# Halving the columns of the backward products with transposed weights

## The chip, the cores and the metric

One core of a Trainium2 chip runs the whole program in one launch. The metric is the device time of that core in microseconds, from the runs below. The core has TensorE (matrix products into PSUM), VectorE, ScalarE, GpSimd, and SyncE, whose queue issues most DMAs. In the profile they are PE, DVE, ACT, POOL and SP; PEld is TensorE's loading of weights, which overlaps its products.

## The reference, cut to what matters

The kernel computes a forward pass and all its gradients. A layer norm of x feeds two branches that are added: a recurrent attention over 64 segments of 32 rows, with 32 heads of 128 and a memory of 8 rows, and a dense layer with a squared ReLU.

```python
mem = mem0
for s in range(n_seg):                       # 64 segments
    h = concatenate([mem, xs], axis=1)       # 8 + 32 rows of 512
    q, k, v = (einsum('btd,dhe->bhte', h, W) for W in (Wq, Wk, Wv))
    p = softmax(where(mask, einsum('bhqe,bhke->bhqk', q, k) * scale, -1e9))
    o = einsum('bhte,hed->btd', einsum('bhqk,bhke->bhqe', p, v), Wo)
    mem = o[:, :M]                           # goes into the next segment
    outs.append(o[:, M:])
out = x + A(layernorm(x)) + B(layernorm(x))
grads = vjp(grad_out)                        # of x, mem0, all weights and biases
```

Backward, the gradient of a segment's memory rows is needed before the segment ahead of it can be begun, so the 64 segments are again a chain. What the change touches is the gradient of h: for each segment the sum over the three projections t and the 32 heads of d(q, k or v) times the transposed weight of that head.

## The kernel before, in words

Four stages follow each other: the dense branch with the layer norm (0 to 330 us of the profile), the forward recurrence with the weight gradients of the dense branch between its steps (to 1390), the backward recurrence (1398 to 2556), and the weight gradients of the attention with the backward layer norm (to the end).

In each of the middle stages the work is handed to a planner (`_Plan`) as operations with an engine or a choice of engines, a cost, the keys that they read and write, and a priority. The planner lists them by cost and due time, and that list is the program order of every engine. Where a choice of ScalarE or VectorE is given, it picks. The costs are written in the code, so a change of costs also moves other operations.

The layout: 32 heads are 8 groups `i` of 4 heads `j` (`JQ`). A segment's q, k, v and their gradients lie with head `j` at partitions 32 j to 32 j + 31, one partition per row. The rows of a segment that take part are 24 new rows and the 8 memory rows, 32 in all; beside them each block of four segments has an L part, the 8 rows of x under each memory, 32 rows in all, which isn't in the chain.

One backward step is `chain(s)`, L1234. `sg.proj` (L405, matmuls at L413) makes gO, the gradient times Wo. gO is transposed by TensorE (gOT). The products dP (L1247) give the gradient of the softmax, which VectorE works out (L1095 to L1106). For t = 2, 1, 0 `part` (L1253) makes the gradient of v, k, q with `diag` (L439, matmuls at L449, 32x32 tiles), ScalarE or VectorE empties it to bf16 (dN), VectorE transposes it in 32x32 blocks (dT, `sq_T`), and `dh_part` (L1108) multiplies with the transposed weights:

```python
for j in range(JQ):
    nc.tensor.matmul(bk()[32 * j:32 * (j + 1), :], lhsT=XT[:, i, j, :],
                     rhs=wtf(t, JQ * i + j), start=(first and i == 0),
                     stop=(last and i == NI - 1), tile_position=(0, 32 * j))
```

Each matmul has 128 rows of contraction, 32 columns of weights and 512 columns of output. The four heads `j` lie in four column groups of TensorE, which run side by side, and leave four partial sums in 32 partitions each of one PSUM bank, ps_dRA: 96 matmuls per step. ScalarE and VectorE copy that bank to SBUF in two halves of 256 columns (R_A, fp32). Then a product in fp32 with `sel8` (L1282), a matrix of ones and zeros, adds the four partial sums and transposes the 8 memory rows at once (ps_gm); VectorE copies the result to gT (PA in the profile), and gO of the next step may start. R_A is also written to memory (S_R, 256 KB per segment); the four partial sums of its other rows are added only in the last stage, in `ln_bwd` (L1380), from ga. In the last step the memory gradient itself is made by an fp32 product (L1289).

The L parts are made once per block of four segments by `l_pre` and `l_post` (L1126, L1162), whose work the planner uses to fill TensorE's waits: gL, dPL, dqL, dL, and `dh_part` again, into ps_dRL, 1,536 matmuls of 512 columns in all, emptied to btL and written to S_RL.

Of the kernel before, what the change touches and what calls it, by code (L numbers as in the profile page):

```python
# [7 lines left out]
ACT = mybir.ActivationFunctionType  # L8
# [9 lines left out]
P = 128  # L18
# [168 lines left out]
def kernel(  # L187
# [99 lines left out]
    S_ONL = dt_([NLC, P, BPC, HW], BF16, "S_ONL")  # L287
    S_GN = dt_([3, TC, P, SPB, HW], BF16, "S_GN")
    S_GNL = dt_([3, NLC, P, BPC, HW], BF16, "S_GNL")
    S_R = dt_([NSEG, P, D], F32, "S_R")  # L290
    S_RL = dt_([TC, P, D], F32, "S_RL")

    ident = const.tile([P, P], BF16, name="ident")
    nc.gpsimd.memset(ident[:], 0.0)
# [2 lines left out]
    )  # L297
    ones_col = const.tile([P, 1], BF16, name="ones_col")
    nc.vector.memset(ones_col[:], 1.0)
    sel8 = const.tile([P, M], F32, name="sel8")  # L300
    nc.gpsimd.memset(sel8[:], 0.0)
    for g in range(JQ):
        nc.gpsimd.affine_select(
            sel8[:], sel8[:], pattern=[[-1, M]], compare_op=ALU.not_equal, fill=1.0, base=-32 * g, channel_multiplier=1
        )
    mean_t = const.tile([P, TC], F32, name="mean_t")
    rstd_t = const.tile([P, TC], F32, name="rstd_t")

# [743 lines left out]
    if True:  # L1052
# [29 lines left out]
        dSTA, dSTL = (pb_rest[:, x * HW // 4:(x + 1) * HW // 4].rearrange("p (i k) -> p i k", i=NI) for x in range(2))  # L1082
        dN = [tl("dN%d" % t, NAT) for t in range(3)]
        dT = [tl("dT%d" % t, TR) for t in range(3)]
        R_A = tl("R_A", [P, D], F32)
        gNat = maskL[:].rearrange("p i k -> p (i k)")

        plan = _Plan(tc, GRACE, AGE, IDLE, KEEP)
# [6 lines left out]
        def smax_bwd(sfx, bk, nk, Ptile, pkey, dSt, dkey, prio, cD):  # L1095
# [9 lines left out]
                                                             op0=ALU.mult, op1=ALU.mult),  # L1105
              [k("bt"), pkey], [dkey], prio)  # L1106

        def dh_part(kind, nm, XT, xk, t, first, last, prio, bk=None):  # L1108
            if bk is None:
                bk = sg.bank(kind, [P, D], F32, "ps_dR" + nm)  # L1110
            for q in range(4):
                def mm(e, q=q):
                    for i in (2 * q, 2 * q + 1):
                        for j in range(JQ):
                            nc.tensor.matmul(bk()[32 * j:32 * (j + 1), :], lhsT=XT[:, i, j, :],  # L1115
                                             rhs=wtf(t, JQ * i + j), start=(first and i == 0),
                                             stop=(last and i == NI - 1), tile_position=(0, 32 * j))
                A(pe(0.435, "w"), mm, [(xk, q // 2)] + [((t, "WT"), g) for g in range(4 * q, 4 * q + 4)], [bk.key], prio)
            return bk

        def dmaT(out_f, in_f, R, W, prio=1):
            A({"SP": 1.5}, lambda e: nc.sync.dma_start_transpose(out_f(), in_f()), R, W, prio, 3.0)
# [39 lines left out]
        def l_post(b):  # L1162
# [52 lines left out]
            order = ((0, LT0), (1, LT1), (2, LT2)) if b else ((0, LT0), (2, LT2), (1, LT1))  # L1215
            for x, (t, L_) in enumerate(order):
                bR = dh_part("f" if b else LKIND, "L", L_, "LT%d" % t, t, x == 0, x == 2, 1, bR)
            sg.evict(lambda: flat(btL), bR, lambda: bR()[:], ["btL"], 1, EV_F)
            sg.dma(lambda: S_RL[b], lambda: flat(btL), ["btL"], [], cost=T_DMA + (b == 0), eng="SP" if b else "POOL")

        def load(s):
            z = s % 2
# [11 lines left out]
        def chain(s):  # L1234
            b, v = s // SPB, s % SPB
            p, z = b % 2, s % 2
            K = lambda n: n + "%d" % p
            both = lambda n: [(n, 0), (n, 1)]
            win = lambda dc: gT[p][:, dc, RA * v:RA * (v + 1)]
            sg.proj("c", "gO", win, [("gT", p), ("gm", p, v), "WB"], wof, 0, ("gN", gN), 0)  # L1240
            sg.to_T_plain("c", "gOT", gN, "gN", gOT, "gOT", 0)
            bk = sg.bank("c", [P, NI, KA], F32, "ps_dP")
            for half in range(2):
                def dp(e, half=half):
                    for i in range(4 * half, 4 * half + 4):
                        for j in range(JQ):
                            nc.tensor.matmul(q_(bk(), j)[:, i, :], lhsT=gOT[:, i, j, :], rhs=VT[:, i, j, :],  # L1247
                                             start=(i == 0), stop=True, tile_position=(0, 32 * j), skip_group_check=True)
                A(pe(0.16, "w"), dp, [("gOT", half), "VT"], [bk.key], 0)
            c0 = RL + M * v  # L1250
            bR = sg.bank("r", [P, D], F32, "ps_dRA")

            def part(t, terms, rk, first, last):  # L1253
                sg.diag("c", "d%d" % t, terms, rk, ("dN%d" % t, dN[t]), 0)
                sg.sq_T(dN[t], "dN%d" % t, dT[t], "dT%d" % t, 0)
                dh_part("r", "A", dT[t], "dT%d" % t, t, first, last, 0, bR)
                sg.dma(lambda: part_of(S_GN[t], s, SPB), lambda: flat(dN[t]), both("dN%d" % t), [])

            part(2, [(lambda j, i: q_(Pt[z], j)[:, i, M:KA], lambda j, i: q_(gN, j)[:, i, :], 32),
                     (lambda j, i: q_(PLL[p], j)[:, i, c0:c0 + M], lambda j, i: q_(gLN[p], j)[:, i, :], M)],  # L1260
                 lambda h: [("Pt", z), ("gN", h), K("PLL"), (K("gLN"), h)], True, False)
            smax_bwd("A", bk, KA, Pt[z], ("Pt", z), dS, "dS", 0, 0.51)
            A({"DVE": 0.1}, lambda e: V.tensor_copy(dSp[v][:, :, M * v:M * (v + 1)], dS[:, :, 0:M]), ["dS"], [("dSp", v)], 0)
            A({"DVE": 0.36}, lambda e: V.transpose(dSTA[:], dS[:, :, M:KA]), ["dS"], ["dSTA"], 0)
            A({"DVE": 0.34}, lambda e: V.transpose(flat(dSTL), dSp[v].rearrange("p i e -> p (i e)")), [("dSp", v)], ["dSTL"], 0)
            part(1, [(lambda j, i: q_(dS, j)[:, i, M:KA], lambda j, i: q_(qN, j)[:, i, :], 32),
                     (lambda j, i: q_(dSL[p], j)[:, i, c0:c0 + M], lambda j, i: q_(qLN[p], j)[:, i, :], M)],
                 lambda h: ["dS", "qN", K("dSL"), K("qLN")], False, False)
            part(0, [(lambda j, i: q_(dSTA, j)[:, i, :], lambda j, i: q_(kN, j)[:, i, :], 32),
                     (lambda j, i: q_(dSTL, j)[:, i, :], lambda j, i: q_(kLN[p], j)[:, i, :], 32)],  # L1270
                 lambda h: ["dSTA", "dSTL", "kN", K("kLN")], False, True)
            for hf in range(2):
                A({"ACT": 0.34, "DVE": 0.4}, lambda e, hf=hf: ev(
                    {"DVE": "v", "ACT": "s"}[e], R_A[:, 256 * hf:256 * hf + 256], bR()[:, 256 * hf:256 * hf + 256]),
                  [bR.key], [("R_A", hf)], 0)
            if s > 0:
                p1, v1 = ((s - 1) // SPB) % 2, (s - 1) % SPB
                bm = sg.bank("c", [P, DC, M], F32, "ps_gm")
                for hf in range(2):
                    def gm(e, hf=hf):  # L1280
                        for dc in (2 * hf, 2 * hf + 1):
                            nc.tensor.matmul(bm()[:, dc, :], lhsT=R_A[:, dc * P:(dc + 1) * P], rhs=sel8[:],  # L1282
                                             start=True, stop=True, skip_group_check=True)
                    A(pe(0.46, "f"), gm, [("R_A", hf)], [bm.key], 0)
                A({"DVE": 0.19}, lambda e: V.tensor_copy(gT[p1][:, :, RA * v1:RA * v1 + M], bm()[:]),  # L1285
                  [bm.key, ("gT", p1)], [("gm", p1, v1)], 0)
            else:
                bm = sg.bank("c", [M, D], F32, "ps_dm0")
                A(pe(0.9, "f"), lambda e: nc.tensor.matmul(bm()[:], lhsT=sel8[:], rhs=R_A[:], start=True, stop=True),  # L1289
                  [("R_A", 0), ("R_A", 1)], [bm.key], 0)  # L1290
                sg.evict(lambda: gNat[0:M, :], bm, lambda: bm()[:], ["gNat"], 0, EV_F)
                sg.dma(lambda: out2flat[:, :], lambda: gNat[0:M, :], ["gNat"], [])
            sg.dma(lambda: S_R[s], lambda: R_A[:], [("R_A", 0), ("R_A", 1)], [])
            sg.dma(lambda: part_of(S_GON, s, SPB), lambda: flat(gN), both("gN"), [("S_GON", s)])
            sg.dma(lambda: part_of(S_DSL, s, SPB), lambda: dSp[v].rearrange("p i e -> p (i e)"), [("dSp", v)], [("S_DSL", s)])

# [64 lines left out]
    with tc.tile_pool(name="p5b", bufs=1) as p5b, tc.tile_pool(name="p5e", bufs=1) as cs1, \  # L1361
# [2 lines left out]
        gbuf += [PA[:], PB[:]] + [p5b.tile([P, HW], BF16, name="gn%d" % x)[:] for x in range(4)]  # L1364
        def ln_in(blk):
            r0 = blk * P
            ga = cs2.tile([P, JQ, D], F32, name="ga4")
            for v in range(SPB):
                s = blk * SPB + v
                dma(ga[RA * v:RA * v + M], S_RL[blk].rearrange("(j r) d -> r j d", r=RL)[M * v:M * (v + 1)])  # L1370
                dma(ga[RA * v + M:RA * (v + 1)], S_R[s].rearrange("(j r) d -> r j d", r=RA)[M:RA])
            gb = cs2.tile([P, D], F32, name="gb4")
            dma(gb[:], S_GXNB[r0:r0 + P, :])
            xnb = cs2.tile([P, D], BF16, name="xnb4")
# [5 lines left out]
        def ln_bwd(blk, ga, gb, xnb, gib):  # L1380
            r0 = blk * P
            V = nc.vector
            s1 = cs1.tile([P, 2, D], F32, name="s14")
            V.tensor_tensor(out=s1[:], in0=ga[:, 0:2, :], in1=ga[:, 2:4, :], op=ALU.add)
            V.tensor_tensor(out=gb[:], in0=gb[:], in1=s1[:, 0, :], op=ALU.add)
            gxn = cs1.tile([P, D], F32, name="gxn4")
            V.tensor_tensor(out=gxn[:], in0=s1[:, 1, :], in1=gb[:], op=ALU.add)
            m1 = cs1.tile([P, 1], F32, name="m1")
            V.tensor_reduce(m1[:], gxn[:], axis=AX.X, op=ALU.add)
            prod = cs1.tile([P, D], BF16, name="prod4")  # L1390
# [106 lines left out]
```

## Time and profile before

| | |
|---|---|
| median of 3 runs | 3132.2 us (3125.16 to 3135.4) |
| profiled execution | 3135.73 us, span 3134.0 us |
| granted TensorE clock | 0.967 |
| TensorE busy | 2817.2 us (90%), 62,681 products |
| VectorE, ScalarE, GpSimd busy | 1542.3, 934.8, 239.1 us |
| DMA | 590.54 MB, 188 GB/s on average |
| L1115, ps_dRA | 6144 matmuls, 380.7 us busy |
| L1282, ps_gm | 504 matmuls in the profile (8 a step) |

Busy times of an engine are unions of its instructions' times, so four matmuls that run side by side count once. A matmul's own duration contains the way through the array; how fast they follow each other is read from their starts. A group's line in the profile has the source line, the engine, what is written from what, shapes and count, then the busy time, the mean duration in ns, and the idle time of the engine just before, with what ended it. "issue" there means that nothing in the profile was waited for.

### The profile page before, as it was taken

What the parts mean: (1) busy time and instruction counts of PE and PEld (TensorE: products, weight loads), DVE (VectorE), ACT (ScalarE), POOL (GpSimd) and SP (SyncE); (2) the same over time, 40 slices, a digit from 0 to 9 for tenths busy, and PEclk for the clock granted to TensorE, in tenths of its full rate; (3) what the DMA queues carried; (4) which work ended last, traced back from release to release, by engine and by line L of the source; (5) the groups of instructions that cost most, each with busy time, mean ns of one, the idle gap of its engine ahead of it and who ended that gap; (6) DMA issues with size and microseconds to landing.
All of it is one profiled execution on the core that took longest, in us unless ns stands there. A gap on an engine that the chain in (4) does not pass through costs nothing.

```text
span 3134.0 us, 138519 instructions
## 1 busy us (share of the span) xinstructions
PE 2817.2 (90%) x62681; PEld 1636.1 (52%) x62847; DVE 1542.3 (49%) x3392; ACT 934.8 (30%) x1807; POOL 239.1 (8%) x402
## 2 busy tenths in 40 slices
PE   8998888888888888888899998999998889999998
PEld 6664555555555555565555555555555544444444
DVE  5544554545444455575555555565655531233322
ACT  4333333434333344333233333333333310000000
POOL 1110000000000000010000000000000001121111
PEclk9999999999999999999999999999999989999999
DMA  6657655555555553256677677787777679788861
GB/s 204 217 162 205 173 150 164 156 158 163 162 158 158 143 160 126 97 129 186 192 194 212 199 199 204 204 215 201 203 204 211 204 227 342 248 249 276 256 184 44
DMA packets 562918, 590.54 MB, mean 188 GB/s; under 512 B 257301, under 2 KB 364006, under 8 KB 560150
## 3 DMA queue, kind: packets, MB, share of 16 engines
q1 hardware_dynamic: 548166, 530.73, 59.3%
q0 software_dynamic: 14096, 50.87, 4.8%
q8 instruction: 491, 8.04, 1.1%
q14 instruction: 101, 0.83, 0.1%
q10 hardware_dynamic: 64, 0.07, 0.0%
HBM read 283.32 MB, written 262.68 MB: 174 GB/s over the span
## 4 chain that ended last, share of the span: by engine, by line
PE 71%; DVE 9%; DMA 8%; issue 6%; SPq 4%; ACT 2%; POOL 0%; ACTq 0%; DVEq 0%; POOLq 0%
PE ps_gw L1444 13%; PE ps_dRA L1115 9%; PE ps_d L449 5%; PE ps_RA L812 4%; PE ps_q L413 3%; PE ps_gw L1448 3%; PE ps_k L413 3%; PE ps_h L607 3%; SPq L359 3%; PE ps_gO L413 2%; PE ps_dRL L1115 2%; PE ps_v L413 2%; PE ps_dw L1007 2%; PE ps_gm L1282 2%; PE ps_o L449 2%
## 5 line engine op out<-in xcount | busy, mean ns | idle before, releaser
L1115 PE MATMUL ps_dRA<-WA,dT 128*32 128x512 bf16 x6144 | 380.7, 388 | 12.7 <-issue 8.6
L413 PEld LDWEIGHTS <-PA 128*32 128x32 bf16 x8192 | 210.5, 100 | 243.2 <-issue 42.7
L1444 PE MATMUL ps_gw<-WA,WB 128*128 128x512 bf16 x1505 | 330.7, 379 | 2.2 <-DVE gwo L315 0.6
L397 DVE STREAM_TRANSPOSE dT<-dN 128x512 bf16<-128x512 bf16 x384 | 256.0, 692 | 96.9 <-ACT dN L317 95.4
L1444 PEld LDWEIGHTS <-WB 128*128 128x128 bf16 x1896 | 185.5, 98 | 225.1 <-issue 2.0
L317 ACT CAST dN<-ps_d 128x512 bf16<-128x512 f32 x357 | 199.1, 587 | 295.5 <-PE ps_d L449 263.8
L1115 PEld LDWEIGHTS <-dT 128*32 128x32 bf16 x6144 | 156.4, 98 | 176.0 <-issue 31.9
L315 DVE CAST gwo<-ps_gw 128x512 bf16<-128x512 f32 x64 | 39.8, 684 | 400.9 <-PE ps_gw L1444 300.3
L812 PE MATMUL ps_RA<-WB,OT 128*32 128x128 bf16 x8192 | 139.3, 223 | 62.1 <-issue 46.7
L317 ACT CAST gwo<-ps_gw 128x512 bf16<-128x512 f32 x64 | 33.0, 600 | 515.3 <-PE ps_gw L1444 357.9
L315 DVE CAST kN<-ps_k 128x512 bf16<-128x512 f32 x120 | 83.0, 692 | 208.2 <-PE ps_k L413 205.3
L413 PE MATMUL ps_q<-WA,PA 128*32 128x512 bf16 x2048 | 165.9, 394 | 10.4 <-DVE PA L949 6.0
L812 PEld LDWEIGHTS <-OT 128*32 128x32 bf16 x8192 | 123.0, 99 | 83.2 <-issue 53.6
L413 PE MATMUL ps_k<-WA,PA 128*32 128x512 bf16 x2048 | 163.8, 390 | 0.8 <-issue 0.5
L449 PEld LDWEIGHTS <-PB 32*32 32x32 bf16 x8192 | 121.3, 94 | 74.6 <-issue 33.1
L413 PE MATMUL ps_gO<-WB,PA 128*32 128x512 bf16 x2048 | 139.4, 418 | 13.4 <-DVE PA L1285 13.1
L1225 POOL COPY bVT<-VR 128x1024 bf16<-128x1024 bf16 x64 | 66.6, 1040 | 971.0 <-PE ps_dP L1247 878.0
L413 PE MATMUL ps_v<-WA,PA 128*32 128x512 bf16 x2048 | 132.6, 388 | 0.0
L317 ACT CAST qN<-ps_q 128x512 bf16<-128x512 f32 x122 | 71.2, 586 | 194.2 <-PE ps_q L413 194.2
L1007 PE MATMUL ps_dw<-sx,anT 128*128 128x512 bf16 x358 | 109.3, 386 | 9.8 <-DMA sx<-in_grad_out_dram 5.4
L397 DVE STREAM_TRANSPOSE OT<-oN 128x512 bf16<-128x512 bf16 x128 | 84.2, 693 | 56.5 <-ACT oN L317 55.2
L1115 PE MATMUL ps_dRL<-WA,LT 128*32 128x512 bf16 x1536 | 107.8, 385 | 1.4 <-ACT dLN L317 1.1
(298 smaller groups left out, 4771.8 us busy)
## 6 DMA issues: line engine op xcount, KB each, us to landing
S_GN<-dN SPq DMA_DIRECT2D x192, 256.0 KB
WA<-S_GN SPq DMA_DIRECT2D x160, 256.0 KB
S_Q<-qN SPq DMA_DIRECT2D x64, 256.0 KB
S_K<-kN SPq DMA_DIRECT2D x64, 256.0 KB
S_V<-vN SPq DMA_DIRECT2D x64, 256.0 KB
S_ON<-oN SPq DMA_DIRECT2D x64, 256.0 KB
bqN<-S_Q SPq DMA_DIRECT2D x64, 256.0 KB
bkN<-S_K SPq DMA_DIRECT2D x64, 256.0 KB
```

Of the source, the lines that this page charges most:

```text
L315: nc.vector.tensor_copy(out, in_)
L317: nc.scalar.copy(out, in_)
L359: self.plan.add({eng: cost}, lambda e: q.dma_start(out_f(), in_f()), R, W, prio, lat)
L397: self.plan.add({"DVE": 0.70}, lambda e, x=x: nc.vector.transpose(dst[:, x, :, :], src[:, x, :].rearrange("p i (a c) -> p i c a", c=JQ)), ...
L413: nc.tensor.matmul(bk()[32 * j:32 * (j + 1), :], lhsT=win(dc), rhs=Wt(dc, c0), start=(dc == 0), stop=(dc == DC - 1), tile_position=(0, 32 ...
L449: nc.tensor.matmul(bk()[32 * j:32 * j + m, k * P:(k + 1) * P], lhsT=lf(j, i), rhs=rf(j, i), start=(k == 0 and x == 0), stop=(x == n - 1), ...
L607: nc.tensor.matmul(bk()[:, x, :], lhsT=Wt[:, dc, fc * P:(fc + 1) * P], rhs=In[:, dc, :], start=(dc == 0), stop=(dc == DC - 1), skip_group_ ...
L812: nc.tensor.matmul(bk()[32 * jd:32 * (jd + 1), :], lhsT=OTt[:, i, j, :], rhs=Wo[:, JQ * i + j, jd * P:(jd + 1) * P], start=(i == 0 and j = ...
L1007: nc.tensor.matmul(bks[x]()[:], lhsT=anT[x][:, c, :], rhs=sx[z][:], start=(c == 0), stop=(c == TC - 1))
L1115: nc.tensor.matmul(bk()[32 * j:32 * (j + 1), :], lhsT=XT[:, i, j, :], rhs=wtf(t, JQ * i + j), start=(first and i == 0), stop=(last and i = ...
L1444: nc.tensor.matmul(bks[n]()[:], lhsT=HNc[:, rc, dc * P:(dc + 1) * P], rhs=gns[y][:, hf * 512:(hf + 1) * 512], start=(y == 0), stop=(y == N ...
L1448: nc.tensor.matmul(bks[n]()[:], lhsT=gns[y][:, k * P:(k + 1) * P], rhs=GOc[:, rc, :], start=(y == 0), stop=(y == NRC - 1))
```

## The change

`dh_part` makes two matmuls of 256 columns for each one of 512. The two column halves `dh` and the parity of the head `j % 2` now choose the column group, so that two heads are added up in PSUM, and the bank has 256 columns with four parts: even and odd heads for each half. `dh_sum` is new: ScalarE copies the odd part (64 partitions) to SBUF in fp32, and VectorE adds it to the even part and writes bf16 (R_S). The memory rows are turned by two TensorE transposes of bf16 in place of the fp32 products. S_R and S_RL are bf16 with 64 rows of 256, and the last stage adds one loaded tile where it added four. In the last step the memory gradient goes out from R_S.

```diff
-    S_R = dt_([NSEG, P, D], F32, "S_R")
-    S_RL = dt_([TC, P, D], F32, "S_RL")
+    DH = D // 2
+    S_R = dt_([NSEG, 2, RA, DH], BF16, "S_R")
+    S_RL = dt_([TC, 2, RL, DH], BF16, "S_RL")
...
+        def hf(t, p):
+            return t[2 * RA * p:2 * RA * (p + 1)]
...
                         for j in range(JQ):
-                            nc.tensor.matmul(bk()[32 * j:32 * (j + 1), :], lhsT=XT[:, i, j, :],
-                                             rhs=wtf(t, JQ * i + j), start=(first and i == 0),
-                                             stop=(last and i == NI - 1), tile_position=(0, 32 * j))
+                            for dh in range(2):
+                                c = 2 * (j % 2) + dh
+                                nc.tensor.matmul(bk()[32 * c:32 * (c + 1), :], lhsT=XT[:, i, j, :],
+                                                 rhs=wtf(t, JQ * i + j)[:, 2 * dh:2 * dh + 2, :],
+                                                 start=(first and i == 0 and j < 2), stop=(last and i == NI - 1 and j >= 2),
+                                                 tile_position=(0, 32 * c))
...
+        def dh_sum(bR, p, prio):
+            A({"ACT": 0.36}, lambda e: nc.scalar.copy(hf(R_2, p), hf(bR(), 1)), [bR.key], [("R_2", p)], prio)
+            A({"DVE": 0.36}, lambda e: V.tensor_tensor(out=hf(R_S, p), in0=hf(bR(), 0), in1=hf(R_2, p), op=ALU.add),
+              [bR.key, ("R_2", p)], [("R_S", p)], prio)
...
-            sg.evict(lambda: flat(btL), bR, lambda: bR()[:], ["btL"], 1, EV_F)
+            dh_sum(bR, 1, 1)
...
-            for hf in range(2):
-                A({"ACT": 0.34, "DVE": 0.4}, lambda e, hf=hf: ev(
-                    {"DVE": "v", "ACT": "s"}[e], R_A[:, 256 * hf:256 * hf + 256], bR()[:, 256 * hf:256 * hf + 256]),
-                  [bR.key], [("R_A", hf)], 0)
+            dh_sum(bR, 0, 0)
             if s > 0:
...
-                bm = sg.bank("c", [P, DC, M], F32, "ps_gm")
-                for hf in range(2):
-                    def gm(e, hf=hf):
-                        for dc in (2 * hf, 2 * hf + 1):
-                            nc.tensor.matmul(bm()[:, dc, :], lhsT=R_A[:, dc * P:(dc + 1) * P], rhs=sel8[:],
-                                             start=True, stop=True, skip_group_check=True)
-                    A(pe(0.46, "f"), gm, [("R_A", hf)], [bm.key], 0)
+                bm = sg.bank("c", [P, 2, 2 * RA], BF16, "ps_gm")
+                def gm(e):
+                    for x in range(2):
+                        transpose_to(bm()[:, x, :], hf(R_S, 0)[:, x * P:(x + 1) * P])
+                A(pe(0.12, "f"), gm, [("R_S", 0)], [bm.key], 0)
...
-            ga = cs2.tile([P, JQ, D], F32, name="ga4")
+            ga = cs2.tile([P, 2, DH], BF16, name="ga4")
...
-            V.tensor_tensor(out=s1[:], in0=ga[:, 0:2, :], in1=ga[:, 2:4, :], op=ALU.add)
-            V.tensor_tensor(out=gb[:], in0=gb[:], in1=s1[:, 0, :], op=ALU.add)
-            V.tensor_tensor(out=gxn[:], in0=s1[:, 1, :], in1=gb[:], op=ALU.add)
+            V.tensor_tensor(out=gxn[:], in0=gb[:], in1=ga[:].rearrange("p h c -> p (h c)"), op=ALU.add)
```

More of the change, by code (lines that the diff above doesn't have):

```diff
@@ L299 @@
     nc.vector.memset(ones_col[:], 1.0)
[L300 to L305, printed above, removed]
     mean_t = const.tile([P, TC], F32, name="mean_t")
@@ L1084 @@
         dT = [tl("dT%d" % t, TR) for t in range(3)]
-        R_A = tl("R_A", [P, D], F32)
+        R_S = tl("R_S", [P, DH])
+        R_2 = tl("R_2", [P, DH], F32)
         gNat = maskL[:].rearrange("p i k -> p (i k)")
@@ L1106, in smax_bwd @@
               [k("bt"), pkey], [dkey], prio)
+        def hf(t, p):
+            return t[2 * RA * p:2 * RA * (p + 1)]
         def dh_part(kind, nm, XT, xk, t, first, last, prio, bk=None):
             if bk is None:
-                bk = sg.bank(kind, [P, D], F32, "ps_dR" + nm)
+                bk = sg.bank(kind, [P, DH], F32, "ps_dR" + nm)
             for q in range(4):
@@ L1217, in l_post @@
                 bR = dh_part("f" if b else LKIND, "L", L_, "LT%d" % t, t, x == 0, x == 2, 1, bR)
-            sg.evict(lambda: flat(btL), bR, lambda: bR()[:], ["btL"], 1, EV_F)
-            sg.dma(lambda: S_RL[b], lambda: flat(btL), ["btL"], [], cost=T_DMA + (b == 0), eng="SP" if b else "POOL")
+            dh_sum(bR, 1, 1)
+            sg.dma(lambda: S_RL[b].rearrange("h r c -> (h r) c"), lambda: hf(R_S, 1), [("R_S", 1)], [],
+                   cost=T_DMA + (b == 0), eng="SP" if b else "POOL")
         def load(s):
@@ L1250, in chain @@
             c0 = RL + M * v
-            bR = sg.bank("r", [P, D], F32, "ps_dRA")
+            bR = sg.bank("r", [P, DH], F32, "ps_dRA")
             def part(t, terms, rk, first, last):
@@ L1271, in chain @@
                  lambda h: ["dSTA", "dSTL", "kN", K("kLN")], False, True)
-            for hf in range(2):
-                A({"ACT": 0.34, "DVE": 0.4}, lambda e, hf=hf: ev(
-                    {"DVE": "v", "ACT": "s"}[e], R_A[:, 256 * hf:256 * hf + 256], bR()[:, 256 * hf:256 * hf + 256]),
-                  [bR.key], [("R_A", hf)], 0)
+            dh_sum(bR, 0, 0)
             if s > 0:
                 p1, v1 = ((s - 1) // SPB) % 2, (s - 1) % SPB
-                bm = sg.bank("c", [P, DC, M], F32, "ps_gm")
-                for hf in range(2):
-                    def gm(e, hf=hf):
-                        for dc in (2 * hf, 2 * hf + 1):
-                            nc.tensor.matmul(bm()[:, dc, :], lhsT=R_A[:, dc * P:(dc + 1) * P], rhs=sel8[:],
-                                             start=True, stop=True, skip_group_check=True)
-                    A(pe(0.46, "f"), gm, [("R_A", hf)], [bm.key], 0)
-                A({"DVE": 0.19}, lambda e: V.tensor_copy(gT[p1][:, :, RA * v1:RA * v1 + M], bm()[:]),
+                bm = sg.bank("c", [P, 2, 2 * RA], BF16, "ps_gm")
[3 more added lines that the diff above has]
+                A(pe(0.12, "f"), gm, [("R_S", 0)], [bm.key], 0)
+                A({"DVE": 0.19}, lambda e: V.tensor_copy(
+                    gT[p1][:, :, RA * v1:RA * v1 + M].rearrange("p (h x) m -> p h x m", h=2),
+                    bm()[:].rearrange("p x (h r) -> p h x r", h=2)[:, :, :, 0:M]),
@@ L1286, in chain @@
                   [bm.key, ("gT", p1)], [("gm", p1, v1)], 0)
             else:
[L1288 to L1293, printed above, removed]
+                for h in range(2):
+                    sg.dma(lambda h=h: out2flat[:, h * DH:(h + 1) * DH], lambda h=h: R_S[RA * h:RA * h + M], [("R_S", 0)], [])
@@ L1294, in chain @@
+            sg.dma(lambda: S_R[s].rearrange("h r c -> (h r) c"), lambda: hf(R_S, 0), [("R_S", 0)], [])
             sg.dma(lambda: part_of(S_GON, s, SPB), lambda: flat(gN), both("gN"), [("S_GON", s)])
@@ L1366, in ln_in @@
             r0 = blk * P
-            ga = cs2.tile([P, JQ, D], F32, name="ga4")
+            ga = cs2.tile([P, 2, DH], BF16, name="ga4")
             for v in range(SPB):
                 s = blk * SPB + v
-                dma(ga[RA * v:RA * v + M], S_RL[blk].rearrange("(j r) d -> r j d", r=RL)[M * v:M * (v + 1)])
-                dma(ga[RA * v + M:RA * (v + 1)], S_R[s].rearrange("(j r) d -> r j d", r=RA)[M:RA])
+                dma(ga[RA * v:RA * v + M], S_RL[blk][:, M * v:M * (v + 1), :].rearrange("h r c -> r h c"))
+                dma(ga[RA * v + M:RA * (v + 1)], S_R[s][:, M:RA, :].rearrange("h r c -> r h c"))
             gb = cs2.tile([P, D], F32, name="gb4")
@@ L1382, in ln_bwd @@
             V = nc.vector
-            s1 = cs1.tile([P, 2, D], F32, name="s14")
-            V.tensor_tensor(out=s1[:], in0=ga[:, 0:2, :], in1=ga[:, 2:4, :], op=ALU.add)
-            V.tensor_tensor(out=gb[:], in0=gb[:], in1=s1[:, 0, :], op=ALU.add)
             gxn = cs1.tile([P, D], F32, name="gxn4")
-            V.tensor_tensor(out=gxn[:], in0=s1[:, 1, :], in1=gb[:], op=ALU.add)
+            V.tensor_tensor(out=gxn[:], in0=gb[:], in1=ga[:].rearrange("p h c -> p (h c)"), op=ALU.add)
             m1 = cs1.tile([P, 1], F32, name="m1")
```

## The prediction

> **What bounds the kernel now.** I read the page first: busy shares and the chain that ended last. Then the three stages as windows, to find the one that the change touches. Then the chain in order of time inside one step of the backward loop, TensorE's waits in that loop, and last the packets of the instruction queue.
>
> The page's chain is made of TensorE work:
>
> ```profile
> PE 71%; DVE 9%; DMA 8%; issue 6%; SPq 4%; ACT 2%; POOL 0%; ACTq 0%; DVEq 0%; POOLq 0%
> ...
> L1115 PE MATMUL ps_dRA<-WA,dT 128*32 128x512 bf16 x6144 | 380.7, 388 | 12.7 <-issue 8.6
> ...
> L812 PE MATMUL ps_RA<-WB,OT 128*32 128x128 bf16 x8192 | 139.3, 223 | 62.1 <-issue 46.7
> ...
> q8 instruction: 491, 8.04, 1.1%
> ```
>
> "issue" is 6% of the span: TensorE stood still with nothing to wait for that the profile knows. The line L812, four times shorter matmuls than L1115, has 46.7 us of it. Keep the queue line for later: 8.04 MB in 491 packets are 16 KB each.
>
> The backward loop is the window 1398 to 2556 us:
>
> ```profile
> 1398.00:2556.00 1158.00, 1037.92 (x29514) 615.68 (x29502) 668.68 (x1329) 366.30 (x677) 89.84 (x138) 0.96 0.73 201
> ```
>
> TensorE is busy 1037.9 of 1158 us, VectorE 668.7, ScalarE 366.3. So TensorE's program order sets the loop's length: 64 steps of 18.1 us. One step's seam (the chain in order of time):
>
> ```profile
> 1953.24 3.57 PE ps_dRA L1115 x64
> 1956.81 0.86 PE ps_dRL L1115 x16
> 1957.68 0.99 PE ps_gm L1282 x8
> 1958.66 0.55 PE ps_gL L413 x8
> 1959.21 1.73 PE ps_gO L413 x32
> ```
>
> 64 dRA matmuls take 3.57 us; then the planner puts other work on TensorE while ScalarE and VectorE empty the bank, then the fp32 product ps_gm, about 1 us, then work again until the next step's ps_gO may start. The waits in the loop:
>
> ```profile
> PE ps_gm L1282 <- DVE R_A L315: 14.0, 9, 3.3
> PE ps_d L449 <- issue: 13.6, 12, 2.0
> PE ps_gO L413 <- DVE PA L1285: 13.1, 27, 2.6
> ...
> PE ps_dRA L1115 <- issue: 8.6, 13, 1.2
> ```
>
> **The seam, 63 times.** Counted from the end of the last dRA matmul, the trace has now: ScalarE's copy at 0.26 us (372 ns), VectorE's copy at 0.66 (419 ns; it already follows ScalarE), first gm at 0.68, or later behind filler, last gm at 1.50 to 1.76, the copy to PA 0.29 after that, gO 0.33 after the copy: 2.1 us with little filler, 2.39 with much. With the change: ScalarE 0.26 to 0.63; VectorE's add 0.66 to 1.08. No row shows that add; the nearest is btA<-ps_dP, 492 ns for 320 columns out of PSUM, so 0.39 for 256; the PSUM copy of the same 256 columns is 0.42, a full fp32 add of 512 is 691 ns; bounds 0.35 to 0.49, I take 0.42. Then two transposes, from gOT's 0.33 us for four: 0.16. PA at 1.48, gO at 1.81. What queues behind the add on VectorE is the copy to PA, in 6 steps with the 0.7 us btL multiply between; there gm no longer hides that multiply and the seam stays at 2.1.
>
> On TensorE 1.06 us of gm (eight at 0.13) become 0.16. The order of the built program says what fills the seam. A typical block of four steps has now 1.29, 1.29, 0.52 and 0.24 us of filler, so TensorE idles 0.03, 0.03, 0.52 and 1.28. After it has 1.73, 1.29, 0.7 and 0.44 us, against 1.81 less 0.16: idle 0, 0.36, 0.95 and 1.21. Work saved 4 x 0.90 = 3.60, idle added 2.52 - 1.86 = 0.66: 2.94 per four steps, **47 us** in 63.
>
> **The halved matmuls.** 6144 + 1536 matmuls of 512 columns become 15,360 of 256. Four column groups run side by side; the start of one matmul to that of the fourth after it is, in the medians, 216 ns at 512 columns (dRA), 56 ns at 128 (ps_RA) and 25 ns at 40 (ps_dP). 216 and 56 are both columns/2.4 plus 2.7 ns, so a round of 256 is 109.4, two of them 2.7 ns more than one of 512: 1,920 rounds, **+5.2 us**. The weight loads are in these periods too: at 128 columns each matmul has its own load of 128x32 and 56 ns are kept, so twice as many loads at 109 ns are not what binds.
>
> The Trainium skill speaks against this term: "TensorEngine Tiling (Array Packing)", section Instruction Overhead, gives each matmul about 60 cycles of overhead. The 2.7 ns of the trace do not bear it out for column groups side by side.
>
> **The program's supply.** TensorE's unexplained pauses in the loop all fall on every 256th of its instructions, without exception, and between two such places there is one 16 KB packet: a block of 256 instructions. 231 blocks pass in the loop. After a block's first instruction its packet starts 1.4 us later (median) and takes 1.1; where TensorE stood still, it went on 1.2 to 1.5 us after the packet's end. So the next block is there about 3.9 us after this one began, and a block that is worked off sooner ends in a pause. The trace bears that out. Blocks by their own working time, pauses taken out: under 3 us 17 blocks, mean pause 1.09; 3 to 3.5: 29, 0.47; 3.5 to 4: 40, 0.33; 4 to 4.5: 40, 0.11; 4.5 to 6: 54, 0.03; over 6: 50, none. Sum 51 us.
>
> The Trainium skill has the mechanism and the opposite verdict: "Runtime: NRT & Kernel Launch", section Instruction fetch mechanics, has 16 KiB blocks fetched while the current one runs, and calls the fetch hidden because dispatch is slower than the fill. The blocks agree with the trace, the hiding does not: 51 us of pauses.
>
> The change adds 15,360 instructions to TensorE (7,680 loads, 7,680 matmuls), takes gm's 1,008 away and adds 252: 59,043 in the loop become 73,650, 288 blocks. I took the trace's instruction times without pauses, put two pairs of half the time for each dRA and dRL pair, shortened gm to what the seam saves, and counted blocks anew: 93, 72, 31, 26, 53 and 11 in the same classes. With the same mean pauses: 101 + 34 + 10 + 3 + 2 = 150 us, **99 us more** than now.
>
> Two things push this size. Up: after a pause the next block took 4.6 us to come, 3.8 otherwise, and pauses will now follow each other. Down: S_R and S_RL shrink from 256 to 32 KB each, so the loop moves some 18 of its 233 MB (201 GB/s) less, and pauses use up waits that are there anyway (ys<-S_PL, 10.6 us in TensorE's waits). I let them cancel.
>
> **Edits with one answer.** The last step's fp32 product and eviction, the 16 evictions of dRL (585 ns, now 372 and about 420 on two engines), the smaller loads of ga and two VectorE adds fewer in the gradient stage (691 ns each, under TensorE's 560 of 578 us there): together 0 to 5 us of gain, I take 4. Issues on SP stay (one S_R per step, 0.32 us; out_2 gets a second). If TensorE were not the cover in the last stage, the VectorE part would be worth 16 x 2.5 us.
>
> **Sum.** The profiled execution took 3135.7 us, span 3134.0, 3.5 above the median of 3132.2. 3135.7 - 47 + 5 + 99 - 4 = 3189; from the median **3185**.
>
> **Rivals.**
> 1. *The supply keeps up, the seam's gain comes through.* One mechanism: the packet is asked for early enough, so that pauses stay at 51 us. For it: four blocks in a row arrived as close as 3.9 us apart, and the changed loop needs one per 3.9. Against it: no eight in a row came closer than 4.26 us on average in this loop, and 288 x 4.26 = 1226 is above 1158. Time: 3132 - 46 = 3086; it decides where added pauses are under 46 us. With half of the 99 us it is a tie, about 3136. By the page of the Trainium skill that calls the fetch hidden it would be this case.
> 2. *The supply becomes the bound.* Nearly every block starts after a pause and takes the 4.6 us seen then: 288 x 4.6 = 1325, loop +167, 3295. For it: 165 of the 288 blocks would be worked off in under 3.5 us. Against it: 90 of the 288 take over 4 us by themselves and let the supply catch up.
> 3. *A fixed cost per round.* If halving cost 25 ns a round in place of 2.7, 1,920 rounds would be +48, and without new pauses 3135: no change. Against it the 56 ns rounds at 128 columns.
>
> That the change does not do what it says is out: the built order has 30,720 matmul and load rows where 15,360 stood, and no fp32 product.
>
> **Numbers.** The measurement tells about 0.3% (9 us) from no change. Forecast (pauses grow by 60 to 150 us): 0.67, own range 3145 to 3240. Supply bound beyond that: 0.11. Tie, rival 3 with it: 0.07. Gain through: 0.15. The range leaves out half of rival 2 and part of rival 1: 3095 to 3260. Faster 0.15, same 0.07, slower 0.78.
>
> **What would show it.** Right: ps_gm at 0.16 us a step in place of 1.06, gO 1.8 us behind the last dRA where filler allows; "issue" ahead of dRA, d and dP in the loop's waits two to three times today's; 288 packets there, 4.2 to 4.4 us apart. Wrong: "issue" in the loop as now, packets regularly under 4 us apart, or a dRA round away from 109 ns.

## The result

The changed kernel takes 3280.3 us in the median of four runs (3264.8 to 3281.7), the kernel before 3133.0: 1.0463 times as long, 95% interval 1.0427 to 1.0500. Slower was forecast, but 53 us of it and not 147; the time lies above the range. It is close to the second rival, in which the supply of instructions becomes the bound (3295).

The page of the changed kernel, the chain that ended last, the two groups of matmuls and the instruction queue:

```profile
PE 71%; issue 11%; DVE 8%; DMA 5%; SPq 2%; ACT 2%; ACTq 0%; POOL 0%; POOLq 0%; DVEq 0%
...
L1117 PE MATMUL ps_dRA<-WA,dT 128*32 128x256 bf16 x12288 | 419.2, 288 | 93.2 <-issue 85.1
...
L807 PE MATMUL ps_RA<-WB,OT 128*32 128x128 bf16 x8192 | 140.1, 224 | 60.3 <-issue 43.9
...
q8 instruction: 548, 8.98, 1.2%
```

"issue" has gone from 6 to 11% of the chain, 491 packets have become 548, and ahead of dRA TensorE stood still 85.1 us for nothing that the profile knows, where it was 8.6. L807, which the change does not touch, is as it was.

The window of the backward loop (busy times of TensorE, its weight loads, VectorE, ScalarE, GpSimd, then clock, DMA share and GB/s):

```profile
1398.00:2712.00 1314.00, 1032.59 (x36886) 779.35 (x36890) 692.48 (x1369) 356.57 (x661) 89.97 (x138) 0.95 0.64 166
```

TensorE is busy as long as before, 1032.6 us, in a window of 1314 us in place of 1158. The waits of TensorE over the whole program (those shown belong to the backward work), us in total, times, longest:

```profile
PE ps_dRA L1117 <- issue: 85.1, 75, 3.3
PE ps_d L444 <- issue: 70.9, 46, 4.1
...
PE ps_dRL L1117 <- issue: 19.5, 17, 2.6
...
PE ps_gm L306 <- DVE R_S L1126: 13.7, 22, 2.3
...
PE ps_gO L408 <- DVE PA L1290: 11.4, 33, 0.8
```

And the chain in order of time through one step, with its seam:

```profile
1984.16 2.59 PE ps_dRA L1117 x65
1986.75 0.86 issue
1987.61 2.69 PE ps_dRA L1117 x92
1990.31 0.56 PE ps_d L444 x32
1990.86 0.17 PE ps_dL L1211 x4
1991.03 1.15 issue
1992.18 0.57 PE ps_dL L1211 x28
1992.76 0.87 PE ps_dRA L1117 x32
1993.63 1.31 PE ps_dRL L1117 x48
1994.94 0.16 PE ps_gm L306 x2
1995.10 0.55 PE ps_dRL L1117 x16
1995.65 0.21 PE ps_gO L408 x2
1995.86 1.99 issue
1997.85 2.25 PE ps_gO L408 x29
```

The fp32 product of about 1 us is 0.16 us now and 32 halved matmuls take 0.87, as worked out. Three standstills within 12 us, in the middle of runs of like matmuls, take 4.0 us. They are the pauses at every 256th instruction.

For all kernels below the trace was counted in the same way: TensorE's instructions from 1398 us to the end of the loop, cut into blocks of 256; a pause is a gap ahead of a block's first instruction that waits for no semaphore and ends with the arrival of the next packet; work is the rest of the loop's time.

| kernel | blocks | work, us | work per block | pauses, us | pause per block |
|---|---|---|---|---|---|
| before | 231 | 1104 | 4.78 | 51 | 0.22 |
| before, second profile | 232 | 1114 | 4.81 | 54 | 0.23 |
| e5_order | 230 | 1079 | 4.66 | 67 | 0.29 |
| e4_bf16seam | 228 | 1076 | 4.72 | 86 | 0.38 |
| e1_seam | 227 | 1075 | 4.70 | 86 | 0.38 |
| s1_noL | 241 | 1013 | 4.20 | 170 | 0.71 |
| e3_tiny | 289 | 1133 | 3.92 | 199 | 0.69 |
| e2_half | 289 | 1103 | 3.83 | 233 | 0.81 |
| changed | 288 | 1067 | 3.68 | 246 | 0.85 |
| s2_dma | 286 | 1024 | 3.58 | 228 | 0.80 |

### The profile page after: what moved, and what is told of

Its sections match the earlier page's. It is cut to its first block, busy times and chain, and to the rows that moved or that the text cites. A ratio compares the mean times of both kernels' runs of the same rounds, so it can differ in the third digit from the quotient of the medians.

```text
span 3279.6 us, 153161 instructions
## 1 busy us (share of the span) xinstructions
PE 2801.7 (85%) x69981; PEld 1797.9 (55%) x70147; DVE 1532.8 (47%) x3395; ACT 922.2 (28%) x1787; POOL 238.4 (7%) x397
## 4 chain that ended last, share of the span: by engine, by line
PE 71%; issue 11%; DVE 8%; DMA 5%; SPq 2%; ACT 2%; ACTq 0%; POOL 0%; POOLq 0%; DVEq 0%
PE ps_gw L1445 12%; PE ps_dRA L1117 11%; PE ps_d L444 6%; PE ps_RA L807 4%; PE ps_gO L408 3%; PE ps_q L408 3%; PE ps_gw L1449 3%; PE ps_h L602 3%; PE ps_k L408 3%; PE ps_dRL L1117 3%; SPq L354 2%; PE ps_v L408 2%; PE ps_dw L1002 2%; PE ps_o L444 2%; PE ps_B L630 1%
## 5 line engine op out<-in xcount | busy, mean ns | idle before, releaser
L1117 PE MATMUL ps_dRA<-WA,dT 128*32 128x256 bf16 x12288 | 419.2, 288 | 93.2 <-issue 85.1
L1117 PEld LDWEIGHTS <-dT 128*32 128x32 bf16 x12288 | 332.9, 102 | 152.8 <-issue 109.3
L807 PE MATMUL ps_RA<-WB,OT 128*32 128x128 bf16 x8192 | 140.1, 224 | 60.3 <-issue 43.9
L807 PEld LDWEIGHTS <-OT 128*32 128x32 bf16 x8192 | 123.9, 99 | 81.3 <-issue 50.8
L408 PE MATMUL ps_gO<-WB,PA 128*32 128x512 bf16 x2048 | 128.3, 391 | 16.0 <-DVE PA L1290 11.4
L1117 PE MATMUL ps_dRL<-WA,LT 128*32 128x256 bf16 x3072 | 110.1, 275 | 19.7 <-issue 19.5
L1126 DVE TENSOR_TENSOR R_S<-ps_dRA,R 64x256 bf16<-64x256 f32 x64 | 26.5, 414 | 191.2 <-ACT R L1125 191.2
```

Source lines behind the costliest of these rows:

```text
L408: nc.tensor.matmul(bk()[32 * j:32 * (j + 1), :], lhsT=win(dc), rhs=Wt(dc, c0), start=(dc == 0), stop=(dc == DC - 1), tile_position=(0, 32 ...
L807: nc.tensor.matmul(bk()[32 * jd:32 * (jd + 1), :], lhsT=OTt[:, i, j, :], rhs=Wo[:, JQ * i + j, jd * P:(jd + 1) * P], start=(i == 0 and j = ...
L1117: nc.tensor.matmul(bk()[32 * c:32 * (c + 1), :], lhsT=XT[:, i, j, :], rhs=wtf(t, JQ * i + j)[:, 2 * dh:2 * dh + 2, :], start=(first and i ...
```

## The experiments

Theory: the added instructions outrun their supply, and the pauses are the whole loss. Rival A: the seam, with VectorE's add behind ScalarE's copy, costs. Rival B: the halving costs by itself, per round or per weight load. e1 to e4 were timed beside the kernel before on one chip (before: 3130.8 us), e5, s1, s2 and the second profile of before on another (before: 3145.9 us). Ratios are to the runs of before on the same chip.

**e1_seam: the seam alone.** The changed kernel, with

```diff
-        for dh in range(2):
-            c = 2 * (j % 2) + dh
-            nc.tensor.matmul(bk()[32 * c:32 * (c + 1), :], lhsT=XT[:, i, j, :],
-                             rhs=wtf(t, JQ * i + j)[:, 2 * dh:2 * dh + 2, :], ...)
+        nc.tensor.matmul(bk()[32 * j:32 * (j + 1), :], lhsT=XT[:, i, j, :], rhs=wtf(t, JQ * i + j), ...)
```

> The changed kernel with matmuls of 512 columns as before, so the seam of the change without its halving. The add takes 256 of the 512 columns and two of the four partial sums' pairs, the rest is left out, so that the seam's instructions are those of the change. Theory (supply of instructions): TensorE has some 750 instructions fewer in the backward loop than before, pauses stay near 51 us, the seam's 47 us come through: 3085 to 3095 us. Rival A (the seam with ScalarE ahead of VectorE is what costs): 3133 or more. Rival B (the halving costs by itself, per round or per weight load): also 3085 to 3095.

3133.1 us, 1.0005 (0.9979 to 1.0030): no change. The theory and rival B had expected the gain of 47 us; rival A names the time that came. The trace shows the gain made and then lost. The seam is as short as in the changed kernel (ps_gO 1.76 us behind the last dRA in the median, 2.39 before), and the work fell by 29 us. The pauses rose by 35. The waits of TensorE in the loop:

```profile
PE ps_d L444 <- issue: 37.8, 27, 3.6
PE ps_d L444 <- DVE maskA L1100: 31.2, 27, 1.9
PE ps_gm L306 <- DVE R_S L1123: 18.0, 23, 3.5
PE ps_dRA L1115 <- issue: 16.4, 14, 2.1
...
PE ps_dRA L1115 <- DVE dT L392: 11.5, 18, 1.4
```

Ahead of ps_d "issue" is 37.8 us, before it was 13.6. The waits for maskA (31.2, before 16.2) and dT (11.5, before 3.6) have grown by 23 us, more than the 18 that the work lacks of the 47: VectorE's chain of four operations behind dP is late next. Rival A's cause, the add behind the copy, is not it: the wait for R_S is 18.0 us, and the waits for R_A were 14.0 for VectorE's half and 7.7 for ScalarE's.

**e2_half: the halving alone.** The kernel before, with

```diff
-    nc.tensor.matmul(bk()[32 * j:32 * (j + 1), :], lhsT=XT[:, i, j, :], rhs=wtf(t, JQ * i + j), ...)
+    for dh in range(2):
+        c = 2 * (j % 2) + dh
+        nc.tensor.matmul(bk()[32 * c:32 * (c + 1), 0:256], lhsT=XT[:, i, j, :],
+                         rhs=wtf(t, JQ * i + j)[:, 2 * dh:2 * dh + 2, :], ...)
```

> The kernel before with halved matmuls and its own seam: the eviction, the fp32 product and the transfers have the instructions and sizes of before, each copying the same 256 columns twice, so the sums are left out. Theory: 15,360 instructions more in the loop, 291 blocks for about 1109 us of work, 3.8 us a block: pauses of 220 to 250 us in place of 51, all at every 256th instruction, time 3290 to 3335. Rival B: the same time, but as longer rounds (over 130 ns) and not as pauses. Rival A: 3140 (1,920 rounds of 2.7 ns).

3311.0 us, 1.0566 (1.0520 to 1.0612). The halving alone costs 180 us. The round of four halved matmuls is 109 ns in the median, not over 130, and the work is that of before, 1103 us. All of the loss is in the pauses, 233 us (the theory had 220 to 250), at every 256th instruction: rival B is out in the form in which it was stated. The changed kernel is 31 us below this one: the seam took 36 us of work off, 13 came back as pauses, and the last stage is shorter (below).

```profile
PE ps_dRA L1117 <- issue: 87.4, 71, 3.7
PE ps_d L449 <- issue: 42.0, 40, 2.2
PE ps_dRL L1117 <- issue: 17.0, 14, 2.3
```

**e3_tiny: the instructions without the halving.** The kernel before, and behind each four matmuls

```diff
+    for j in range(JQ):
+        nc.tensor.matmul(bk()[32 * j:32 * (j + 1), 0:8], lhsT=XT[:, i, j, :],
+                         rhs=wtf(t, JQ * i + j)[:, 0, 0:8], start=False, ...)
```

> The kernel before, matmuls of 512 columns and the old seam, but after each four of them four more of 8 columns with their own weight loads, which count 8 columns twice. It adds the same 15,360 instructions as the halving and nothing is halved. A round of four small ones costs at most the 25 ns that the shortest rounds show: 1,920 x 25 = 48 us. Theory: work 1104 + 48 = 1152 us for 291 blocks, 3.96 us a block, pauses 170 to 230 us: 3290 to 3360. Rival B (the halving costs by itself): 3181 at most. Rival A: 3181 at most.

3305.4 us, 1.0539 (1.0484 to 1.0595). Nothing is halved, each matmul has its 512 columns, the seam is the old one, and the loss is as large. The work rose by 29 us, the pauses to 199 (the theory had 170 to 230), and they stand ahead of both kinds of matmul (L1115 has 512 columns, L1119 has 8):

```profile
PE ps_dRA L1115 <- issue: 40.9, 37, 3.6
PE ps_d L449 <- issue: 37.2, 36, 2.1
PE ps_dRA L1119 <- issue: 31.5, 31, 3.0
```

So the number of instructions in the time decides, not what they are. Both rivals had 3181 at most.

**s1_noL: fewer instructions elsewhere.** The changed kernel without the second term of each `part`:

```diff
-    part(2, [(... Pt[z] ..., 32), (lambda j, i: q_(PLL[p], j)[:, i, c0:c0 + M], ..., M)], ...
+    part(2, [(... Pt[z] ..., 32)], ...
```

> The changed kernel with the second terms of the three products of each step (the L parts in part) left out: 12,288 instructions fewer on TensorE in the loop and about 97 us of its work, halved matmuls and seam as changed. Theory: 240 blocks for about 970 us of work, 4.0 us a block and the densest stretches gone, pauses from 246 to 90 to 150 us: 3050 to 3130. Rival (the halving costs by itself): only the work goes, 3280 - 97 = 3183.

3149.7 us, 1.0013 (0.9988 to 1.0038): 20 us above the theory's span, 33 below rival B's time, on a chip where before took 13 us longer than the 3133 that both start from. The work fell by 54 us only, since TensorE now waits for VectorE (R_S 30.8 us, dT 25.8). The pauses fell by 76 us to 170; the theory had 90 to 150. Why they stay that high shows in the blocks: 72 of 241 are worked off in 3 to 3.5 us. A block made of halved rounds alone is 256 / 8 x 0.109 = 3.5 us, shorter than the 3.8 us that the next block takes to come when there was no pause before; with 512 columns it is 6.9. The halved stretch doesn't need the dense neighbours to run out of instructions, and it has stopped being the place where the supply caught up.

**s2_dma: less data on the DMA engines.** The changed kernel without

```diff
-    sg.dma(lambda: part_of(S_GN[t], s, SPB), lambda: flat(dN[t]), both("dN%d" % t), [])
```

> The changed kernel without the writes of S_GN (192 of 256 KB, 50 MB in the loop, a quarter of its traffic); the last stage reads S_Q in their place. TensorE's instructions stay 73.8 thousand in the loop. If the data on the DMA engines hold up the instruction packets, the packets start sooner than 1.6 us after a block's start and pauses fall by 50 us or more: 3180 to 3240. If the time to fetch a block is its own, pauses stay within 20 us of 246: 3260 to 3285.

3221.5 us, 1.0263 (1.0224 to 1.0302). The time falls between the two expectations. The pauses are 228 us, 18 fewer, with a quarter of the traffic gone. A packet starts 1.56 us after its block in the mean, in place of 1.62. Most of the gain is in the work, 1024 us in place of 1067. Half of that, 21 us, is waits of TensorE for others, most of it in the seam (before these lines R_S was 13.7 and PA 11.4):

```profile
PE ps_gO L408 <- DVE PA L1289: 6.8, 19, 0.7
...
PE ps_gm L306 <- DVE R_S L1126: 2.9, 5, 0.9
```

The other half is TensorE's busy time, 1012 us in place of 1033, at a granted clock of 0.96 in the loop in place of 0.95. The 18 us are not the whole price of the traffic: the blocks became shorter as well, 3.58 us of work in place of 3.68, and shorter blocks have longer pauses in the table above.

What the data traffic does to a packet shows inside one trace. In the changed kernel, after 46 of the blocks that began with a pause the 16 DMA engines were less than 30% busy with data for the next 1.5 us, and the next packet started 1.14 us after the block (median). After 56 they were over 95% busy, and it was 2.21 us. In s2_dma these are 67 blocks with 1.15 us and 38 with 2.47. So a packet comes about 1 us later where data fill the DMA engines, though no run here changes that alone.

**e4_bf16seam and e5_order: the seam's gain without the instructions.** Both keep 512 columns and leave nothing out; the product in the seam is bf16:

```diff
-    sel8 = const.tile([P, M], F32, name="sel8")
+    sel8 = const.tile([P, M], BF16, name="sel8")
...
-        R_A = tl("R_A", [P, D], F32)
+        R_A = tl("R_A", [P, D])
```

with S_R, S_RL and ga in bf16 as well. e4 gives the planner the shorter costs (0.46 to 0.12 for each half of the product), e5 leaves the costs, so TensorE's order is that of before.

> A version meant to keep the seam's gain without the instructions: matmuls of 512 columns, R_A, sel8, S_R and S_RL in bf16, so that the sum and transposition of the memory rows is a bf16 product of four matmuls in place of the fp32 one. Theory: gm from 1.06 to about 0.33 us a step, 504 instructions fewer in the loop, pauses at 51 us or a little less: 3090 to 3105 us. Rival A: 3133, since the two copies of the bank still follow each other. Rival B has no part in it: 3090 to 3105.

3147.4 us, 1.0051 (1.0030 to 1.0072): 0.5% longer, where all theories had 3090 to 3133. Its ten runs had a granted clock of 0.965 to 0.970, those of before beside them 0.969 to 0.975, and the five of before at 0.969 or 0.970 took 3135 to 3151 us; so it is not shown that e4 is slower at the same clock, only that the gain didn't come. Its work is 1076 us, 28 less than before, its pauses are 86 us, and ps_d waits 45.9 us for maskA.

> The bf16 product in the seam again, matmuls of 512 columns, with the planner's costs of the kernel before, so that TensorE's order is that of before, instruction kind by instruction kind, and only the product in the seam is shorter. Theory (work saved at the same instruction count is given back as pauses): work in the loop 30 to 40 us less, pauses 20 to 35 us more than the 51 of before, time 3115 to 3135. Rival (the new order of the planner brought the pauses and the waits for maskA): pauses stay at about 51, time 3090 to 3105.

3118.1 us, 0.9924 (0.9897 to 0.9951): 0.8% faster than before, with the interval clear of 1; by the ratio that is 24 us under the kernel before. Four bf16 matmuls stand where eight fp32 ones stood:

```profile
L1283 PE MATMUL ps_gm<-sel,R_A x252: 166/168/189, 1420.8 to 2527.6; 128*128 128x8 bf16 x126
```

The work is 1079 us, about that of e4, but pauses are 67 us and the wait for maskA is 16.1 as before. The second profile of before, below, is of the same chip: against it the work is 35 us less and the pauses are 13 us more, which makes 22 of the 24 us. So the expectation's two sides each had a part: some 13 to 16 us of the work saved came back as pauses, fewer than the 20 to 35 expected. The other 19 that e4 has came with the planner's new order, for the planner's costs are all that e4 and e5 differ in, apart from the chip they ran on. For e1, also at 86 us, the same is likely but not shown.

**b2_before: the kernel before again.**

> The kernel before once more, for a second profile: how far the pauses of 51 us and the 231 blocks repeat. All theories: 3120 to 3150; pauses within 15 us of 51 if a difference of 35 us in one profile is to be read as one of the kernel.

3149.6 us; 232 blocks, 53.5 us of pauses. The pauses repeat within 3 us, so the 86 of e1 and e4 and the 67 of e5 are read as theirs. The work repeats within 10 us only (1104 and 1114).

## Why the prediction was right in its mechanism and wrong in its size

**The seam** held. ps_gO starts 1.75 us behind the last dRA (median; predicted 1.81), the add takes 414 ns (0.42), the two transposes 0.16. The work of the loop fell from 1104 to 1067 us; 42 us were predicted.

**The halved matmuls** held: 109 ns a round, predicted 109.4.

**The blocks** held: 288 of them, and by their working time 90, 67, 37, 20, 63 and 10 in the six classes, where 93, 72, 31, 26, 53 and 11 were counted from the trace of before.

**The pauses per class** are the term that was mis-sized, 99 us more where 195 came. The sum took the mean pauses of before. In the changed kernel the same classes have 1.46 us (1.09 before), 1.15 (0.47), 0.51 (0.33), 0.39 (0.11) and 0.18 (0.03). With these and the predicted counts the sum is 254 us, and 246 were measured: the counts were good, the means were not. One reason is that a block that began after a pause waits longer for its successor: 4.43 us after a pause (165 cases), 3.81 otherwise (122). Before, 46 of 230 blocks began so and 50 had over 6 us of work in which to recover; now it is more than half, and 10 recover. The prediction saw this ("after a pause the next block took 4.6 us to come") and let it cancel against the lighter DMA traffic and the waits. The cancelling was the wrong step. s2_dma gives a size for the other side: 18 us of pauses for a quarter of the traffic, where the change took off 8%.

How far this goes can be worked out. Take the mean pauses of the two profiles of before by class and also by whether the block began after a pause. For the blocks of the changed kernel they give 204 us; by class alone they give 155, and 247 came in the same count. For e2_half it is 227 of 234, for e3_tiny 184 of 198. Before has only 14 such blocks with under 4 us of work, so these sums are rough: the repeated pauses make up about half of what the changed kernel's sum missed, and the rest stays open.

The fetch rule of the Trainium skill that the prediction named ("Runtime: NRT & Kernel Launch", section Instruction fetch mechanics: hidden behind the dispatch) fails further: 0.85 us stood open per block in the changed kernel.

**The rivals.** The second decided, nearly: it had every block after a pause at 4.6 us, 1325 us of loop; 1314 came, 4.56 us a block on average. But only 165 of 288 blocks began after a pause, so the closeness is in part luck. The first was rejected on its best eight packets in a row (4.26 us apart); the changed loop's best eight are 3.98 apart, so that argument was weaker than it looked, but the loop's average never came near the 3.9 that it needed. The third is out by the round of 109 ns.

**Edits with one answer** gave more than the 0 to 5 us: from the loop's end the last stage takes 568 us, 579 before. e1_seam, with the same small S_R, has 571, e4 and e5 with 128 KB have 578 and 579.

**The signs.** ps_gm at 0.16 us, gO at 1.8 us and the round of 109 ns came. "issue" was to be two to three times as large; ahead of dRA it is ten times (8.6 to 85.1 us), ahead of d five times (13.6 to 70.9), and the packets are further apart than the 4.2 to 4.4 us named.

**Small slips of the working**, which change nothing in the outcome: 2.94 us in four steps are 46 us in 63, not 47. Rival 3 adds up to 3129 us (3132 - 47 + 48 - 4), not 3135. The idle 1.28 us of the fourth step belongs to a seam of 2.58 us, which the trace has there and the working doesn't list. The 6% of "issue" is a share of the chain that ended last, in which SyncE's short issue times count too, and not of TensorE's time.

What stays open: why a block that begins after a pause waits longer for the next. In the changed kernel its packet starts 1.9 us after it (mean) in place of 1.2. The DMA engines are busier with data behind such a start, 68% of the next 1.5 us in place of 55%, but that is not all of it: where they are less than 30% busy the packet starts 1.14 us after such a block and 0.67 after another, where they are over 95% busy 2.21 and 1.79 (medians). Open is also what costs e1 and e4 some 20 us of pauses at the same number of blocks. The packets of both start later after a pause, 2.3 us where before and e5 have 2.0 (means), in some 60 cases each; the cause is not known.

## What to carry to other kernels

Where a chain on TensorE looks bound by work, count its instructions per microsecond as well: here every 256 of them must last about 4 us, and matmuls that are split cost their packets even where the array takes them at the same rate. Pauses are not to be summed from means of a program that seldom pauses, because one pause makes the next likelier; and work that is cut from such a loop at the same number of instructions comes back in part as pauses. A shorter operation can be worth more with the old cost in a planner than with its true one: compare the orders before the costs are corrected.

## What the runs showed of the hardware that was not expected

No two instruction packets of TensorE came closer than 3.28 us in any of the loops measured, and no eight in a row closer than 3.83 us on average (s2_dma), whatever the instructions in them were. A packet itself takes 1.1 us (median) in all of them. Ten loops with 3.6 to 4.8 us of work per block lie near one falling line of pause against work per block (the table above), from 0.22 to about 0.85 us; the best straight line misses none by more than 0.13 us, s1_noL by the most. And in each of them the packet starts later the busier the DMA engines are with data in the 1.5 us behind the block's start (correlation 0.45 to 0.66).
